# A fused attention, mixture-of-experts and MLP kernel: exponentials written in place, low parts on GpSimd with waits, joined flat copies, and the first entry's coarse values by four products each

## The chip, the cores and the metric

One NeuronCore of a Trainium2 chip runs the whole program in one launch. The metric is the device time of that launch in microseconds. Three runs of the kernel before gave 1092.92, 1094.10 and 1094.66 us; the median is 1094.1 us. The profile shown below is one further execution.

## The reference, cut to what matters

```python
def _attn_ref(q, k, v):                       # 2 x 8 x 576 x 64
    q_d, k_d, v_d = (x.reshape(B, H, S // 4, 4, D).mean(axis=3) for x in (q, k, v))
    out_up = np.repeat(sm_attn(q_d, k_d, v_d), 4, axis=2)      # coarse
    scores = np.where(abs(i - j) < 4, scale * q @ k.T, -1e9)   # local
    return out_up + softmax(scores) @ v

def _moe_ref(x, w_gate, w1, w2):              # 1152 x 512, 8 experts, 1024 wide
    P = exp(x @ w_gate - max); eight rounds of row and column normalisation
    return sum(P[:, e:e + 1] * (np.maximum(x @ w1[e], 0) @ w2[e]) for e in range(8))

def _moe2_ref(x, w_in, w_out):                # 512 -> 2048 -> 512
    h = x @ w_in
    return (maximum(h, 0) + log1p(exp(-abs(h)))) @ w_out
```

The three are chained: the attention's output, laid out as 1152 tokens of 512, goes through the experts and then through the MLP. The MLP's weights come as 64-bit floats and are taken apart by integer operations on the chip.

## The kernel before, in words

**Attention.** The 16 pairs of batch entry and head are worked in eight units of two heads (`units`, L452): four for the first entry (`self.b == 0`), then four for the second. A unit has four blocks: "c" (the coarse attention, all of it) and 0, 1, 2 (a third of the local attention each). The loop at L741 walks over the stream of 32 blocks: `scores` of block n, then `turn` (transposes of the exponentials) of block n-2, then `values` of block n-3. At the third and fourth block of a unit, `setup` (L313) of the next unit runs: nine TensorE transposes of q and k, sums of four neighbours for the coarse q and k (L327), the scaled coarse q (`flat`, L333, two pieces for each of three groups), and copies into `kT` and `fine`. After the last of them, `load` issues the q, k, v transfers of the unit after that, all on SyncE's one queue. The tile of q and k (`qk`) and that of v for the coarse part (`vd`) have one buffer each, so a load waits until the last reader of the unit before is done.

**Coarse values.** In `setup`, for every unit, GpSimd adds the four neighbours of v (L346, L347) into `vs`, and `values("c")` (L413) multiplies the turned exponentials with `vs`, in two halves of the 144 coarse keys and for two heads: four products. The two heads go to different halves of the output's partitions.

**Exponentials.** In `scores` ScalarE reads a block's scores from PSUM, writes the exponentials to a tile `ex` in SBUF and their sums to `rs` in SBUF (L379, three a block); VectorE adds a small constant to the sums (L380), inverts them (L381) and multiplies `ex` in place (L382).

**Expert weights.** Each float32 weight or activation is split into a high and a low part, and a product is made of three products of parts. The first layer goes by a scheme of seven products in place of eight, so that for each weight tile four sums of weights are needed (`weight_sums`, L105) as well as the plain pieces. `fetch_first` (L113) loads a tile into `raw` (two buffers for all weight loads), ScalarE writes the high parts, VectorE the low parts of the plain pieces (L133), GpSimd the four sums (L111) and their low parts (L139). `fetch_second` (L141) does the second layer's, with the low parts on GpSimd (L154). The first three pairs of fetches (f = 0, 1, 2) fall into the attention stage (L747), the rest are spread over the expert stage.

**Experts beside attention, and after it.** From the second entry's units on, the first four steps of the first expert (`beside`, L714) are woven in between the blocks. After the attention, TensorE's order is fixed by hand (L791); the other engines' order, and everything in the attention stage, is set by a scheduler from the dependencies. Later on `convert` (L161) makes the MLP's weights float32 and uses the same `weight_sums`.

## Time and profile before

| | |
|---|---|
| median of three runs | 1094.1 us |
| profiled execution, span from first to last instruction | 1094.7 us |
| TensorE busy | 1060.0 us (97%) |
| VectorE busy | 727.0 us (66%) |
| ScalarE busy | 555.2 us (51%) |
| GpSimd busy | 537.6 us (49%) |
| mean granted TensorE clock | 0.979 |

The profiled execution's only recorded time is its span, 1094.7 us; it is 0.6 us over the median of the runs and 0.04 us over the longest of them. All times below are microseconds from the span's start. [...] In the stretches from 160 us on TensorE is busy nearly all the time. It is not so before 90 us, which is the attention of the first batch entry.

### The profile page before, as it was taken

To read this page: it belongs to the slowest core of one execution; us is meant where nothing else is said; L and a number is where in the kernel's file an instruction comes from. 1 tells how busy PE (TensorE), PEld (TensorE's weight loads), DVE (VectorE), ACT (ScalarE), POOL (GpSimd) and SP (SyncE) were. 2 spreads that over 40 slices of the span, in tenths; PEclk is the share of its full clock that TensorE was granted. 3 is DMA by queue.
4 is the path that set the end of the run, shared out by engine and by line. 5 is a ranking of instruction groups with operands and counts; after the bars stand their busy time and mean duration, and the time that the engine had idled before them with its cause. 6 is when DMAs were issued, how large, how long until landed. Compare 5 with 4: busy or idle time off the path is not lost.

```text
span 1094.7 us, 17873 instructions
## 1 busy us (share of the span) xinstructions
PE 1060.0 (97%) x6385; PEld 938.0 (86%) x6385; DVE 727.0 (66%) x1532; ACT 555.2 (51%) x1443; POOL 537.6 (49%) x569
## 2 busy tenths in 40 slices
PE   6899999999999999999999999999999998999998
PEld 5678888998987889888888988898898897889987
DVE  6889665565666676667657665766663578766765
ACT  4667645343444444434444443444443567676763
POOL 6735235464467676756766455354664212222321
PEclk9579999999999999999999999999999999999999
DMA  8454101111235334434443332223333273244112
GB/s 175 118 115 109 49 27 55 62 58 40 84 100 145 115 110 143 132 105 127 122 134 102 117 112 93 100 93 110 102 116 116 106 278 139 113 175 182 68 39 87
DMA packets 133497, 119.70 MB, mean 109 GB/s; under 512 B 35744, under 2 KB 111776, under 8 KB 133408
## 3 DMA queue, kind: packets, MB, share of 16 engines
q1 hardware_dynamic: 133408, 118.56, 35.0%
q8 instruction: 50, 0.82, 0.3%
q14 instruction: 39, 0.32, 0.1%
HBM read 93.11 MB, written 25.43 MB: 108 GB/s over the span
## 4 chain that ended last, share of the span: by engine, by line
PE 40%; POOL 5%; DMA 5%; DVE 3%; issue 2%; ACT 2%; SPq 0%; POOLq 0%; ACTq 0%; DVEq 0%
PE yps L660 21%; PE m L601 19%; DMA raw<-in_moe_w_out 2%; POOL sums L111 2%; POOL w2l L154 1%; POOL cva L188 1%; POOL cva L197 1%; DMA raw<-in_moe_w 1%; DMA raw<-in_moe_w_in 1%; DVE cva L178 1%; POOL w1l L139 1%; DVE cva L189 0%; DVE cva L179 0%; DVE cva L182 0%; DMA s_out<-cva 0%
## 5 line engine op out<-in xcount | busy, mean ns | idle before, releaser
L601 PE MATMUL m<-xh,w1h 128*128 128x320 f32 (+1 forms) x1120 | 336.6, 301 | 13.1 <-ACT t L610 6.3
L601 PE MATMUL m<-xh,w1l 128*128 128x320 f32 (+1 forms) x1120 | 332.5, 297 | 0.0
L601 PE MATMUL m<-xl,w1h 128*128 128x320 f32 (+1 forms) x1120 | 332.4, 297 | 0.0
L601 PEld LDWEIGHTS m<-xh,w1h 128*128 128x128 f32 x1120 | 212.2, 189 | 38.7 <-ACT t L610 10.8
L601 PEld LDWEIGHTS m<-xl,w1h 128*128 128x128 f32 x1120 | 212.4, 190 | 11.8
L601 PEld LDWEIGHTS m<-xh,w1l 128*128 128x128 f32 x1120 | 212.2, 190 | 0.2 <-issue 0.2
L660 PE MATMUL yps<-w2h,hh 128*128 128x512 f32 x502 | 198.5, 395 | 0.0
L660 PE MATMUL yps<-w2l,hh 128*128 128x512 f32 x502 | 198.4, 395 | 0.0
L660 PE MATMUL yps<-w2h,hl 128*128 128x512 f32 x502 | 195.5, 389 | 0.0
L660 PE MATMUL yps<-w2h,h 128*128 128x512 f32 x436 | 153.3, 393 | 0.0
L615 DVE TENSOR_TENSOR c<-m,t 128x256 f32<-128x256 f32 (+1 forms) x160 | 72.3, 452 | 100.9 <-PE m L601 99.5
L139 POOL TENSOR_TENSOR w1l<-sums,w1h 128x512 fp32r<-128x512 f32 x72 | 95.8, 1345 | 78.2 <-ACT w1h L138 54.4
L571 POOL TENSOR_TENSOR ab<-ab,up 128x320 f32<-128x320 f32 (+1 forms) x64 | 53.9, 843 | 157.2 <-ACT ln L567 109.8
L154 POOL TENSOR_TENSOR w2l<-raw,w2h 128x512 fp32r<-128x512 f32 x72 | 94.9, 1339 | 71.4 <-ACT w2h L153 71.3
L558 ACT ACTIVATE hh<-c 128x256 fp32r<-128x256 f32 (+1 forms) x138 | 60.0, 443 | 125.0 <-DVE c L615 123.3
L559 DVE SCALAR_TENSOR_TENSOR hl<-c,hh 128x256 fp32r<-128x256 f32 (+1 forms) x138 | 91.4, 668 | 35.0 <-ACT hh L558 33.2
L660 PEld LDWEIGHTS yps<-w2h,hl 128*128 128x128 f32 x502 | 94.4, 188 | 21.3
L677 DVE SCALAR_TENSOR_TENSOR acc<-yps,pr,acc 128x512 f32<-128x512 f32 x117 | 86.9, 743 | 29.5 <-PE yps L660 29.4
L660 PEld LDWEIGHTS yps<-w2h,hh 128*128 128x128 f32 x502 | 94.7, 189 | 12.6 <-DVE acc L673 0.2
L660 PEld LDWEIGHTS yps<-w2l,hh 128*128 128x128 f32 x502 | 94.7, 189 | 11.1 <-issue 0.4
L660 PEld LDWEIGHTS yps<-w2h,h 128*128 128x128 f32 x436 | 82.6, 189 | 14.8
L188 POOL TENSOR_TENSOR cva<-cva,raw 128x512 uint32<-128x512 uint32 x32 | 42.7, 1336 | 95.2 <-DVE raw L185 76.6
(134 smaller groups left out, 1700.7 us busy)
## 6 DMA issues: line engine op xcount, KB each, us to landing
raw<-in_moe_w SPq DMA_DIRECT2D x72, 256.0 KB
raw<-in_moe_w SPq DMA_DIRECT2D x36, 512.0 KB
w1h<-s_in SPq DMA_DIRECT2D x10, 896.0 KB
w1l<-s_in SPq DMA_DIRECT2D x10, 896.0 KB
raw<-in_moe_w_in SPq DMA_DIRECT2D x32, 256.0 KB
raw<-in_moe_w_out SPq DMA_DIRECT2D x16, 512.0 KB
w2l<-s_out SPq DMA_DIRECT2D x10, 512.0 KB
w2h<-s_out SPq DMA_DIRECT2D x10, 512.0 KB
```

Of the source, the lines that this page charges most:

```text
L111: nc.gpsimd.tensor_tensor(sums[i], a, b, op=op)
L139: nc.gpsimd.tensor_tensor(lo[:, part], sums, hi[:, part].bitcast(F32), op=ALU.subtract)
L154: nc.gpsimd.tensor_tensor(lo[:, i], raw[:, i], hi[:, i].bitcast(F32), op=ALU.subtract)
L178: nc.vector.tensor_scalar(a, high, 0x07FFFFFF, 3, op0=ALU.bitwise_and, op1=ALU.logical_shift_left)
L188: nc.gpsimd.tensor_tensor(a, a, low, op=ALU.add)
L558: nc.scalar.activation(hh, c, AF.Relu)
L559: nc.vector.scalar_tensor_tensor(out=hl, in0=c, scalar=0.0, in1=hh.bitcast(F32), op0=ALU.max, op1=ALU.subtract)
L571: nc.gpsimd.tensor_tensor(ab, ab, up, op=ALU.subtract)
L601: nc.tensor.matmul(b[:, :h], x[:, i, kk, :], y[s][:, i, kk, :], start=(not more and n == 0), stop=(n == 5), skip_group_check=more,)
L615: nc.vector.tensor_tensor(c, b[:, :h], t, op=ALU.add)
L660: nc.tensor.matmul(y, a[:, f, tok], b[:, f, :], start=(start and m == 0), stop=(stop and m == 5))
L677: nc.vector.scalar_tensor_tensor(out=acc[t], in0=y, scalar=pr[:, t, e : e + 1], in1=acc[t], op0=ALU.mult, op1=ALU.add,)
```

## The change: what it does

- **Exponentials in place.** ScalarE writes the exponentials back to the PSUM bank of the scores, and their sums to three spare columns of the same bank. VectorE reads both from PSUM: the sum plus constant (L380) and the multiplication (L382), which now goes from PSUM to `ex` in SBUF.
- **Low parts on GpSimd.** For the first three fetches the low parts of the plain pieces (L133) go from VectorE to GpSimd.
- **Waits.** The helper `after` makes every GpSimd instruction of a fetch, or of a set of sums, depend on the one before it in a list, so that it waits for its completion.
- **Joined flat copies.** The six pieces of `flat` become two, made after the third group.
- **Coarse values.** For the first entry's four units the GpSimd sums are left out; `values("c")` takes the four neighbours of `vd` as they are, with sixteen products in place of four.

```diff
+    def after(chain, ins):
+
+        if chain:
+            tc.add_manual_dep(
+                ins.ins, chain[-1], mybir.DependencyInfo(mybir.DependencyClass.Sync, mybir.DependencyReason.DATA)
+            )
+        chain.append(ins.ins.name)
+
+    def weight_sums(sums, w, chain):
...
-            nc.gpsimd.tensor_tensor(sums[i], a, b, op=op)
+            after(chain, nc.gpsimd.tensor_tensor(sums[i], a, b, op=op))
...
+        chain = []
         for part, src in (
...
             nc.scalar.copy(hi[:, part], src)
-            nc.vector.tensor_tensor(lo[:, part], src, hi[:, part].bitcast(F32), op=ALU.subtract)
+            low = (nc.gpsimd if f < 3 else nc.vector).tensor_tensor(
+                lo[:, part], src, hi[:, part].bitcast(F32), op=ALU.subtract
+            )
+            if f < 3:
+                after(chain, low)
...
-            nc.gpsimd.tensor_tensor(lo[:, part], sums, hi[:, part].bitcast(F32), op=ALU.subtract)
+            after(chain, nc.gpsimd.tensor_tensor(lo[:, part], sums, hi[:, part].bitcast(F32), op=ALU.subtract))
...
-            nc.gpsimd.tensor_tensor(lo[:, i], raw[:, i], hi[:, i].bitcast(F32), op=ALU.subtract)
+            after(chain, nc.gpsimd.tensor_tensor(lo[:, i], raw[:, i], hi[:, i].bitcast(F32), op=ALU.subtract))
...
-            for hh in range(2):
+            for hh in range(2 if g == NB - 1 else 0):
                 half = slice(hh * D, (hh + 1) * D)
                 nc.vector.tensor_scalar(
-                    self.flat[half, g, hh].rearrange("x (j g) -> x j g", j=NB), qkd[half, tiles, 0],
+                    self.flat[half, :, hh].rearrange("x i (j g) -> x i j g", j=NB),
+                    qkd[half, :, 0].rearrange("x (i j) g -> x i j g", i=NB),
                     SCALE / (R * R), None, op0=ALU.mult,
                 )
...
-            if g:
+            if g or self.b == 0:
                 return
...
+            total = sc[:rows, NB * SD : NB * SD + NB].rearrange("p (i s) -> p i s", s=1)
             for i in range(NB):
-                nc.scalar.activation(ex[:, i], scv[:, i], AF.Exp, bias=off[:, i], accum_out=rs[:, i])
-            nc.vector.tensor_scalar(rs, rs, EPS, None, op0=ALU.add)
+                nc.scalar.activation(scv[:, i], scv[:, i], AF.Exp, bias=off[:, i], accum_out=total[:, i])
+            nc.vector.tensor_scalar(rs, total, EPS, None, op0=ALU.add)
             nc.vector.reciprocal(rs, rs)
-            nc.vector.tensor_tensor(ex, ex, rs.to_broadcast([rows, NB, w]), op=ALU.mult)
+            nc.vector.tensor_tensor(ex, scv, rs.to_broadcast([rows, NB, w]), op=ALU.mult)
...
-                    for c in range(2):
+                    terms = [
+                        (c, self.vd[:, c, hh, r] if self.b == 0 else self.vs[:, c, hh])
+                        for c in range(2) for r in range(R if self.b == 0 else 1)
+                    ]
+                    for n, (c, vals) in enumerate(terms):
                         nc.tensor.matmul(
-                            pv[hh * D : (hh + 1) * D, :SD], self.vs[:, c, hh],
+                            pv[hh * D : (hh + 1) * D, :SD], vals,
```

The scheduler orders the attention stage anew. On SyncE's queue (`qk`, `vw`, `vd` are a unit's q and k, its windows of v and its v for the coarse part; `raw` is expert weights) the kernel before has, from the load for the third unit's coarse v to that of the fifth unit's q:

```order
L311 DMA vd<-in_v 72x2x256
L298 DMA qk<-in_q 64x9x64 x2
L298 DMA qk<-in_k 64x9x64 x2
L311 DMA vd<-in_v 72x2x256
L124 DMA raw_1207<-in_moe_w 128x4x128 x2
L124 DMA raw_1258<-in_moe_w 128x4x128 x2
L304 DMA vw<-in_v 72x2x64 x2
L308 DMA vw<-in_v 72x7x64 x2
L311 DMA vd<-in_v 72x2x256 x2
```

and the changed kernel, for the same stretch, where L132, L312, L318, L322 and L325 are the lines that were L124, L298, L304, L308 and L311:

```order
L132 DMA raw_1262<-in_moe_w 128x4x128 x2
L312 DMA qk<-in_q 64x9x64 x2
L312 DMA qk<-in_k 64x9x64 x2
L318 DMA vw<-in_v 72x2x64 x2
L322 DMA vw<-in_v 72x7x64 x2
L132 DMA raw_1482<-in_moe_w 128x4x128 x2
L325 DMA vd<-in_v 72x2x256 x2
```

The fourth unit's q and k, which stood ahead of the third and fourth weight loads (raw_1207, raw_1258), now stand behind both (raw_1262 is the second of them), and the third unit's coarse v behind a fifth.

On TensorE the kernel before has, around the second unit's products (L413; L322 are the transposes of `setup`, L355 the coarse scores, L402 the turning of the local exponentials):

```order
L322 MATMUL tb<-ident,qk 128x128 x3
L413 MATMUL pv<-etc,vs 64x144
L402 MATMUL tp<-ident,ex 72x128 x3
L413 MATMUL pv<-etc,vs 64x144 x3
L362 LDWEIGHTS identb
L362 MATMUL sc<-mask,identb 128x216
L355 MATMUL sc<-qkd,flat_149 96x144 x2
```

and the changed kernel, around the second unit's sixteen products (L433, before L413; L336 are the transposes of `setup`, before L322; L370 the coarse scores; L444 the local values):

```order
L370 MATMUL sc<-qkd,flat_149 96x144 x3
L418 MATMUL tp<-ident,ex 72x128 x3
L377 LDWEIGHTS identb
L377 MATMUL sc<-mask,identb 128x216
L383 MATMUL sc<-kT,fine_147 128x72 x3
L433 MATMUL pv<-etc,vd 64x144 x16
L336 MATMUL tb<-ident,qk 128x128 x6
L444 MATMUL pv<-et,vw 64x64 x6
```

The products of the second unit now stand behind the third unit's coarse scores (L370), and directly ahead of the fourth unit's transposes; before they stood ahead of those scores.

On GpSimd the kernel before works the second fetch (raw_778 the first layer's tile, w2l<-raw_969 the second layer's) so:

```order
L111 TENSOR_TENSOR sums<-raw_778 128x256 x2
L347 TENSOR_TENSOR vs<-vd 72x128 x2
L111 TENSOR_TENSOR sums<-raw_778,sums 128x256
L154 TENSOR_TENSOR w2l<-raw_969,w2h 128x512 x2
L111 TENSOR_TENSOR sums<-raw_778,sums 128x256
```

and the changed kernel (raw_977 is now the second layer's) so:

```order
L142 TENSOR_TENSOR w1l<-raw_778,w1h 128x256
L152 TENSOR_TENSOR w1l<-sums,w1h 128x512
L142 TENSOR_TENSOR w1l<-raw_778,w1h 128x512
L168 TENSOR_TENSOR w2l<-raw_977,w2h 128x512
L119 TENSOR_TENSOR sums<-raw_778 128x256
L168 TENSOR_TENSOR w2l<-raw_977,w2h 128x512
L119 TENSOR_TENSOR sums<-raw_778 128x256
L119 TENSOR_TENSOR sums<-raw_778,sums 128x256 x2
```

The two low parts that were VectorE's (L142) now stand ahead of the sums of the tile (L119), which are its last readers; the sums of v (L347) are gone.

## Rows read from the trace of the kernel before

**Rows 1.** Page, costliest groups: form and count, then busy us, mean ns, idle before.

```profile
L139 POOL TENSOR_TENSOR w1l<-sums,w1h 128x512 fp32r<-128x512 f32 x72 | 95.8, 1345 | 78.2 <-ACT w1h L138 54.4
```

**Rows 2.** Windows: stretch, length, busy (instructions) of PE, PEld, DVE, ACT, POOL, clock, DMA.

```profile
25.20:32.00 6.80, 5.52 (x67) 4.54 (x66) 6.56 (x20) 5.53 (x26) 6.80 (x9) 1.00 0.66 179
32.00:66.20 34.20, 29.91 (x175) 23.82 (x175) 29.99 (x78) 21.46 (x84) 22.33 (x28) 0.50 0.61 127
66.20:79.80 13.60, 11.54 (x124) 10.03 (x123) 9.16 (x35) 9.99 (x46) 1.88 (x4) 0.99 0.48 92
79.80:86.60 6.80, 6.55 (x35) 5.86 (x36) 6.71 (x24) 3.51 (x14) 1.40 (x2) 0.52 0.34 77
86.60:160.00 73.40, 72.46 (x608) 61.71 (x606) 56.01 (x148) 48.30 (x175) 31.82 (x32) 1.00 0.26 64
160.00:900.00 740.00, 730.07 (x4235) 651.05 (x4234) 467.30 (x864) 324.71 (x731) 406.50 (x400) 1.00 0.34 109
```

**Rows 3.** Waits from 0 to 110 us: who waited for whom, us, times, longest.

```profile
PE tp L393 <- DVE ex L382: 3.3, 3, 2.2
PE tp L402 <- DVE ex L382: 1.3, 2, 1.1
PE tp L402 <- DVE small L380: 1.3, 1, 1.3
```

**Rows 4.** Timeline of PE: start, us, engine, line, operation, idle before.

```profile
19.82 1.24 PE L413 MATMUL pv<-etc,vs 72*64 72x144 f32 x8
...
46.62 1.49 PE L322 MATMUL tb<-ident,qk 128*128 128x128 f32 x6
...
63.40 1.49 PE L322 MATMUL tb<-ident,qk 128*128 128x128 f32 x6
...
70.19 0.72 PE L413 MATMUL pv<-etc,vs 72*64 72x144 f32 x8
...
78.43 0.85 PE L322 MATMUL tb<-ident,qk 128*128 128x128 f32 x6 [2.06 <-DMA qk<-in_k]
```

**Rows 5.** Lines by form, DVE, 19 to 66 us: busy us, mean ns.

```profile
L382 DVE TENSOR_TENSOR ex<-ex,small 128x216 f32<-128x216 f32 x9 | 8.0, 901 | 0.1
...
L133 DVE TENSOR_TENSOR w1l<-raw,w1h 128x256 fp32r<-128x256 f32 x3 | 3.8, 1252 | 0.0
L380 DVE TENSOR_SCALAR small<-small 128x3 f32<-128x3 f32 x8 | 3.4, 424 | 0.0
L382 DVE TENSOR_TENSOR ex<-ex,small 96x432 f32<-96x432 f32 x3 | 3.1, 1022 | 0.1
...
L133 DVE TENSOR_TENSOR w1l<-raw,w1h 128x512 fp32r<-128x512 f32 x3 | 2.4, 798 | 0.0
L439 DVE TENSOR_TENSOR xf<-pv,xc 128x192 f32<-128x192 f32 x7 | 2.4, 339 | 1.4 <-PE pv L424 1.3
```

**Rows 6.** Timeline of DVE: the same multiplication twice.

```profile
33.54 3.70 DVE L382 TENSOR_TENSOR ex<-ex,small 128x216 f32<-128x216 f32 x1
...
39.53 0.37 DVE L382 TENSOR_TENSOR ex<-ex,small 128x216 f32<-128x216 f32 x1
```

**Rows 7.** Timeline of POOL: a run at 34 us, and sums without and with waits.

```profile
33.83 2.48 POOL L154 TENSOR_TENSOR w2l<-raw,w2h 128x512 fp32r<-128x512 f32 x2
...
388.08 1.44 POOL L111 TENSOR_TENSOR sums<-raw 128x256 f32<-128x256 f32 x2 [2.12 <-DMA s_in<-cva]
389.48 1.56 POOL L111 TENSOR_TENSOR sums<-raw,sums 128x256 f32<-128x256 f32 x2
```

**Rows 8.** Timeline of SP: issues of transfers.

```profile
35.45 1.28 SPq L298 DMA_DIRECT2D qk<-in_q  x2
...
38.83 2.04 SPq L124 DMA_DIRECT2D raw<-in_moe_w  x4
...
71.57 1.29 SPq L298 DMA_DIRECT2D qk<-in_q  x2
```

**Rows 9.** Timeline of ACT: an instruction and one that waits for it.

```profile
891.18 0.47 ACT L564 ACTIVATE ab<-c 128x320 f32<-128x320 f32 x1 [0.99 <-DVE c L615]
891.69 0.47 ACT L565 ACTIVATE ab<-ab 128x320 f32<-128x320 f32 x1
```

More of the change, by code (lines that the diff above doesn't have):

```diff
@@ L103, in attention_moe_mlp @@
     weights = {}
-    def weight_sums(sums, w):
+    def after(chain, ins):
[5 more added lines that the diff above has]
+    def weight_sums(sums, w, chain):
         for i, a, b, op in (
@@ L132, in fetch_first @@
             nc.scalar.copy(hi[:, part], src)
-            nc.vector.tensor_tensor(lo[:, part], src, hi[:, part].bitcast(F32), op=ALU.subtract)
+            low = (nc.gpsimd if f < 3 else nc.vector).tensor_tensor(
[3 more added lines that the diff above has]
+                after(chain, low)
         two = [smp.tile([P, 2, 2, P], F32, tag="sums", name="sums") for _ in range(2)]
-        weight_sums([two[i // 2][:, i % 2] for i in range(SUMS)], lambda fh, d: raw[:, d, :, fh, :])
+        weight_sums([two[i // 2][:, i % 2] for i in range(SUMS)], lambda fh, d: raw[:, d, :, fh, :], chain)
         for i, sums in enumerate(two):
@@ L151, in fetch_second @@
         nc.sync.dma_start(raw, w2[e].rearrange("(h a p) d -> p h a d", h=2, p=P)[:, :, p, :])
+        chain = []
         for i in range(2):
             nc.scalar.copy(hi[:, i], raw[:, i])
-            nc.gpsimd.tensor_tensor(lo[:, i], raw[:, i], hi[:, i].bitcast(F32), op=ALU.subtract)
+            after(chain, nc.gpsimd.tensor_tensor(lo[:, i], raw[:, i], hi[:, i].bitcast(F32), op=ALU.subtract))
     TINY = 2.0 ** -15 * 1.125
@@ L210, in convert @@
         sums = smp.tile([P, SUMS, P], F32, tag="sums", name="sums")
-        weight_sums([sums[:, i] for i in range(SUMS)], lambda fh, d: a[:, 2 * d + fh])
+        weight_sums([sums[:, i] for i in range(SUMS)], lambda fh, d: a[:, 2 * d + fh], [])
         parts(sums, first[:, :SUMS], nc.gpsimd)
@@ L411, in values @@
                 for hh in range(2):
-                    for c in range(2):
+                    terms = [
[3 more added lines that the diff above has]
+                    for n, (c, vals) in enumerate(terms):
                         nc.tensor.matmul(
-                            pv[hh * D : (hh + 1) * D, :SD], self.vs[:, c, hh],
+                            pv[hh * D : (hh + 1) * D, :SD], vals,
                             et[:, c].rearrange("s (i h q) -> s i h q", i=NB, h=2)[:, :, hh],
-                            start=(c == 0), stop=(c == 1),
+                            start=(n == 0), stop=(n == len(terms) - 1),
                         )
```

## The prediction

> **What bounds the kernel now.** I read the stretches first, because the shares of the whole span hide where TensorE has room. From 160 to 900 us it is busy for 730.1 of 740.0 us, and from 86.6 to 160 for 72.5 of 73.4, at the full clock [rows 2]: there nothing that other engines do can give back more than a few microseconds. Room is before 86.6 us, in the first entry's four units. There the clock matters as much as the gaps. From 25.2 to 32.0 it was granted in full; then, after TensorE had waited 2.2 us in one piece for VectorE's multiplication of the exponentials [rows 3], it stood at half from 32.0 to 66.2, though TensorE was busy for 29.9 of those 34.2 us; and it fell again at 79.8, after a wait of 2.06 us for q and k [rows 2, 4]. The waits say what was late: TensorE's transposes waited for L382 and L380 on VectorE, 3.3 + 1.3 + 1.3 = 5.9 us in all [rows 3].
>
> Why is VectorE late? The same multiplication took 3.70 us at 33.54 and 0.37 us at 39.53 [rows 6]. During the first, GpSimd ran without a break, two low parts of 2.48 us among them [rows 7]. Nine of these took a mean of 901 ns, three coarse ones 1022, and eight additions to three numbers 424 ns each, while a VectorE operation that reads its tensor from PSUM beside one in SBUF (L439) kept to 339 ns in the same stretch [rows 5]. So VectorE loses time where it works on SBUF alone while GpSimd does.
>
> **In-place exponentials.** Twelve multiplications took 8.0 + 3.1 = 11.1 us between 19 and 66 us. Undisturbed they would take 9 x 0.37 + 3 x 0.74 (the coarse ones have twice the columns) = 5.6. Reading PSUM they should not be disturbed, as L439 is not, so 5.5 us go. Eight additions of 3.4 us drop at least to 8 x 0.34 = 2.7, another 0.7 [rows 5]. The cost is on ScalarE: three exponentials of a block share one bank now, and two of the three wait for the one before. A waiting instruction starts 0.51 us after the start of one that takes 0.47 [rows 9], so a wait costs 0.04 us and the overlap of neighbours; I bound it by 0.04 and 0.3 (most of a short instruction), 8 a unit, 0.3 to 2.4 us, and take 1. The bank of scores is also held until VectorE has multiplied; with three banks in turn I cost that at nothing, and its cover is that a bank comes round again only three blocks later.
>
> **Low parts on GpSimd.** VectorE loses 3.8 + 2.4 = 6.2 us over three fetches [rows 5]. GpSimd gains 0.72 us for the narrow one (half of 1.44 [rows 7]) and 1.35 for the wide one [rows 1], 2.07 a fetch. Together with the last part, VectorE is rid of 5.5 + 0.7 + 6.2 = 12.4 us in 47, which is 2.8 units of 16.8 us (63.40 less 46.62 [rows 4]), so 4.4 us a unit. It had 29.99 of 34.2, or 14.7 a unit [rows 2], and comes to 10.3. The joined flat copies take a little more off; I put them at nothing, since VectorE is then not the last.
>
> As disturbed as it is here, VectorE needed 1.25 + 0.80 = 2.05 us for the two [rows 5], just what GpSimd needs. [...]
>
> **The waits on GpSimd.** Two sums without a wait between took 1.44 us, two with one 1.56 [rows 7], so a wait costs 0.12 us. Some 120 are new over the whole program, about 15 us of an engine that is half idle. Behind it TensorE is full [rows 2]; I take 0, with ends of -1 (breaks that VectorE can use) and +2.
>
> **Sixteen products.** Eight passes (four products) took 1.24 us at the lower clock and 0.72 at the higher [rows 4]. The difference, 0.52, is their streaming at the full clock, and 0.2 is latency. Sixteen take 4.2 us at half and 2.1 at full, so a unit gains 3.1 or 1.6 us of TensorE, if the two heads still run side by side as in that row, where they write different halves of the partitions; if not, 7.3 or 3.6. I take side by side. What goes in return, the sums of v on GpSimd, nobody on TensorE waited for long.
>
> **The pace of a unit.** ScalarE needs 21.46 / 34.2 x 16.8 = 10.5 us plus 1. TensorE needs 29.91 / 34.2 x 16.8 = 14.7 at half, 17.8 with the products; at full half of 14.7 plus 1.6, 8.9 [rows 2]. So at the higher clock a unit could take 11.5 (ScalarE), at the lower 17.8 (TensorE). The long waits for VectorE ahead of the fall of the clock go, and a block of 4 us without gaps comes in, so I expect the higher clock most of the time: with a third of the units' time at half, 17.8 / 3 + 11.5 x 2 / 3 = 13.6 in place of 16.8.
>
> **The queue it is moved past.** The fourth unit's q and k, issued at 35.45 ahead of the weights at 38.83 [rows 8], now stand behind those weights, whose buffer is free only when GpSimd has read the second weight tile. If GpSimd is no later than before they issue at 38.83 + 2.04 = 40.9; with two fetches' low parts (4.1) and eight waits (1.0) more, at 46.0; the dropped sums of v give some back, so I take 42.5. From issue to use such a load took 78.43 - 71.57 = 6.9 us when TensorE waited for it [rows 4, 8]. So these transposes come at 49.4 (bounds 47.8 and 52.9) where they stood at 46.62, 2.8 us later. From there the pace of 13.6 gives the fifth unit's at 63.0 (before 63.40) and the sixth's at 76.6 (before 78.43), 1.8 us ahead. From then on TensorE has the experts' products beside and is the bound; so what is gained there stays.
>
> **Sum.** Sixth unit -1.8; the second fall of the clock at 79.8, which cost half of 6.55 us busy [rows 2], 3.3, goes if the wait for q and k ahead of it does, and I take -3; waits 0. That is -4.8 on the span of 1094.7, 1089.9; the median of the runs lies 0.6 lower, so **1089 us**, with 1085 to 1092 as this case's own range.
>
> **Rivals.**
> 1. *Slower: the clock stays at half and the added products are the path.* Eight tenths of the stretch from 32.0 to 66.2 was busy TensorE at half [rows 2], and the clock did not rise for being busy. Then a unit takes 17.8: the sixth unit's transposes come at 49.4 + 35.6 = 85.0, 6.6 us late, giving 1100; if the two heads run one after the other, 22 a unit, 1109. It decides if the clock is at half for more than about two thirds of the time from 32 to 66 us. Against it: the longest waits go.
> 2. *No change: the load queue takes the place of VectorE.* With GpSimd slower at its new work, weight buffers come free late, and q, k and v stand behind them on the one queue: TensorE waits for transfers where it waited for VectorE. At the late bound, 52.9, and 13.6 a unit, the sixth unit's come at 80.1, 1.7 late, against a smaller loss of clock: 1094. For it: 2.06 us were waited for a q and k load already [rows 4]. [...]
> 3. *A larger gain.* The clock stays up from 25 us on and the queue is not late: 46.6 + 2 x 11.5 = 69.6, 8.8 us early, and 3.3 for the later fall: 1082.
> 4. *It does not do what it says:* the exponentials' waits on each other and the banks held longer take from ScalarE and TensorE what VectorE gains; about 1095.
>
> **Chances.** A measurement of this kernel tells about 0.2%, 2.2 us, from no change. Forecast 0.42, larger gain 0.14, the queue 0.20, the clock at half 0.20, not as it says 0.04. Faster: 0.42 + 0.14 + 0.03 (the better edge of the queue's case) = 0.59; the same: most of the queue's and the last case, 0.19; slower: 0.22. The range goes from the larger gain, 1082, to the clock's case, 1100; outside are some of both ends, under 0.2 in all.
>
> **What would show it.** Right: L382 near 0.4 us throughout the attention stage and no wait of TensorE for it over 1 us; more than half of 32 to 66 us at the higher clock; the sixteen products in some 2 us at the higher clock; the sixth unit's transposes near 77 us. Wrong: TensorE waiting for q, k or `vd` transfers for several us before 60 (second rival), or busy at half to 66 us and beyond (first rival), or a stretch after 160 us that differs by over 2 us, which I have at nothing.

## The result, and the profile after

The changed kernel is slower: 1106.4 us (median of four runs, 1099.81 to 1114.35) beside 1094.4 for the kernel before, a ratio of 1.0109 (95%: 1.0083 to 1.0136). Six later runs gave 1.0082 (1.0050 to 1.0115). Ratios rest on fast runs alone and are not quotients of the medians beside them, which take in every run. I had 1089, with 1100 as the upper end. Not only the middle moved: the runs spread over 14.5 us where those of the kernel before spread over 4.4.

The profiled run happens to be the fastest of the four (1099.81, span 1098.0), so it shows what the change does at its best. Measured times stand 1.8 us above the span in every run; the profiled execution of before was therefore one of 1096.5, 2.4 above the median shown, not 0.6 as I had put it.

Totals on the page of the changed kernel:

```profile
PE 1062.6 (97%) x6481; PEld 942.4 (86%) x6481; DVE 706.5 (64%) x1494; ACT 557.8 (51%) x1443; POOL 540.6 (49%) x559
```

VectorE is rid of 20.5 us (727.0 before), TensorE has 96 instructions more (6385 before). The same stretches as in [rows 2], columns as there:

```profile
25.20:32.00 6.80, 6.80 (x31) 5.46 (x31) 0.00 (x0) 2.37 (x6) 4.69 (x5) 1.00 0.67 169
32.00:66.20 34.20, 30.04 (x289) 26.78 (x290) 23.66 (x83) 26.49 (x111) 18.80 (x20) 0.95 0.57 127
...
79.80:86.60 6.80, 6.60 (x69) 5.42 (x67) 6.12 (x18) 5.25 (x20) 3.20 (x5) 1.00 0.71 156
...
160.00:900.00 740.00, 727.07 (x4208) 647.32 (x4207) 468.49 (x858) 323.20 (x724) 415.37 (x400) 1.00 0.34 107
```

VectorE fell from 29.99 to 23.66 us between 32 and 66 us, as intended. But TensorE was busy for 6.80 of 6.80 us from 25.2 on, and VectorE did nothing there at all: TensorE's own work holds up the rest. The fall of the clock at 80 us is gone (1.00 where [rows 2] have 0.52). Between 160 and 900 us it has 3.0 us less work done than before.

TensorE's timeline of the changed kernel (start, us, line, operation; in brackets the idle time ahead) shows what that work is:

```profile
23.49 2.18 PE L433 MATMUL pv<-etc,vd 72*64 72x144 f32 x8
...
26.39 5.12 PE L433 MATMUL pv<-etc,vd 72*64 72x144 f32 x24
...
44.00 1.48 PE L370 MATMUL sc<-qkd,flat 128*96 128x144 f32 x6 [2.25 <-DVE flat L347]
...
46.09 1.43 PE L383 MATMUL sc<-kT,fine 128*128 128x72 f32 x6
47.45 3.83 PE L433 MATMUL pv<-etc,vd 72*64 72x144 f32 x32
51.20 0.87 PE L336 MATMUL tb<-ident,qk 128*128 128x128 f32 x6
...
53.29 0.80 PE L383 MATMUL sc<-kT,fine 128*128 128x72 f32 x6
...
59.07 3.70 PE L433 MATMUL pv<-etc,vd 72*64 72x144 f32 x32
62.70 0.87 PE L336 MATMUL tb<-ident,qk 128*128 128x128 f32 x6
...
70.78 3.70 PE L433 MATMUL pv<-etc,vd 72*64 72x144 f32 x32
77.09 0.87 PE L336 MATMUL tb<-ident,qk 128*128 128x128 f32 x6
```

The sixteen products (32 passes, L433) took 2.18 + 5.12 = 7.3 us in the first unit and 3.70 in the third and fourth. I had 4.2 and 2.1. The longest wait between 20 and 110 us is a new one, 2.25 us for the joined flat copy (L347). The six products of `kT` (L383) are a clock to read by: 1.43 us at the lower level, 0.80 at the higher. That is needed, since the first record of the clock in this trace stands at 34.1 us and is one of the higher level; ahead of it the clock column says 1.00, as it does for 25.2 to 32.0, though the products of `kT` took 1.43 us just ahead of that stretch, at 21.49, and the coarse scores (L370) at its end, at 31.44, took 1.76, beside 0.98 at 57.10.

Two numbers per trace carry the rest: **H**, how long the clock stood at its lower level up to 168 us (all of the time ahead of the first record, checked by those products, and the records after it), and **E**, the start of the 223rd product of the experts' first line (L601 before, L621 after), behind which every kernel has the same TensorE work in the same order. Span less E is what a profile took for that work. For the kernel before H is 66 us and E 168.7; for this profile of the change 37 and 166.0.

### The profile page after: what moved, and what is told of

Its sections match the earlier page's. It is cut to its first block, busy times and chain, and to the rows that moved or that the text cites. A ratio compares the mean times of both kernels' runs of the same rounds, so it can differ in the third digit from the quotient of the medians.

```text
span 1098.0 us, 18045 instructions
## 1 busy us (share of the span) xinstructions
PE 1062.6 (97%) x6481; PEld 942.4 (86%) x6481; DVE 706.5 (64%) x1494; ACT 557.8 (51%) x1443; POOL 540.6 (49%) x559
## 4 chain that ended last, share of the span: by engine, by line
PE 55%; POOL 12%; DVE 8%; DMA 6%; issue 5%; ACT 3%; SPq 1%; POOLq 0%; DVEq 0%; ACTq 0%
PE yps L680 27%; PE m L621 25%; POOL sums L119 5%; DMA raw<-in_moe_w_in 2%; POOL w2l L168 2%; POOL cva L211 2%; DMA raw<-in_moe_w_out 2%; DVE cva L193 2%; POOL w1l L152 1%; POOL cva L202 1%; DVE cva L203 1%; DMA raw<-in_moe_w 1%; DVE cva L196 1%; DVE hl L579 1%; DMA s_in<-cva 1%
## 5 line engine op out<-in xcount | busy, mean ns | idle before, releaser
L621 PE MATMUL m<-xh,w1h 128*128 128x320 f32 (+1 forms) x1120 | 337.0, 301 | 16.6 <-ACT t L630 8.9
L621 PE MATMUL m<-xl,w1h 128*128 128x320 f32 (+1 forms) x1120 | 332.7, 297 | 0.0
L621 PE MATMUL m<-xh,w1l 128*128 128x320 f32 (+1 forms) x1120 | 332.0, 297 | 0.0
L621 PEld LDWEIGHTS m<-xh,w1h 128*128 128x128 f32 x1120 | 212.3, 190 | 43.5 <-ACT t L630 12.9
L621 PEld LDWEIGHTS m<-xl,w1h 128*128 128x128 f32 x1120 | 212.5, 190 | 11.8
L621 PEld LDWEIGHTS m<-xh,w1l 128*128 128x128 f32 x1120 | 212.3, 190 | 0.3 <-issue 0.2
L152 POOL TENSOR_TENSOR w1l<-sums,w1h 128x512 fp32r<-128x512 f32 x72 | 101.2, 1406 | 60.8 <-ACT w1h L151 32.5
L579 DVE SCALAR_TENSOR_TENSOR hl<-c,hh 128x256 fp32r<-128x256 f32 (+1 forms) x138 | 86.7, 632 | 40.6 <-ACT hh L578 38.5
L680 PE MATMUL yps<-w2l,h 128*128 128x512 f32 x218 | 86.1, 395 | 0.0
```

The lines of the kernel that those rows point to most:

```text
L152: after(chain, nc.gpsimd.tensor_tensor(lo[:, part], sums, hi[:, part].bitcast(F32), op=ALU.subtract))
L579: nc.vector.scalar_tensor_tensor(out=hl, in0=c, scalar=0.0, in1=hh.bitcast(F32), op0=ALU.max, op1=ALU.subtract)
L621: nc.tensor.matmul(b[:, :h], x[:, i, kk, :], y[s][:, i, kk, :], start=(not more and n == 0), stop=(n == 5), skip_group_check=more,)
L680: nc.tensor.matmul(y, a[:, f, tok], b[:, f, :], start=(start and m == 0), stop=(stop and m == 5))
```

## Experiments

Each ratio is to runs of the kernel before on the same chip. Their median was 1096.9 us for no_waits, sums_back, heads_in_turn and sums_back_no_waits; 1096.2 for products_alone, exps_flat, waits_alone and change_again; 1097.0 for waits_early, waits_late, change_early_waits and before_again; 1097.2 for half_products, products_alone_turn, low_alone and no_products_early; 1096.9 for fewer_buffers and v_twice. H and E, in us, are of one profiled execution each.

| kernel | median us | ratio (95%) | H | E |
|---|---|---|---|---|
| before_again | 1096.4 | 0.9995 (0.9974 to 1.0016) | 65 | 167.5 |
| change_again | 1106.1 | 1.0082 (1.0050 to 1.0115) | 52 | 174.8 |
| no_waits | 1118.6 | 1.0218 (1.0179 to 1.0258) | 79 | 190.1 |
| sums_back | 1099.8 | 1.0031 (1.0012 to 1.0050) | 77 | 168.2 |
| sums_back_no_waits | 1099.7 | 1.0025 (1.0001 to 1.0049) | 55 | 166.7 |
| heads_in_turn | 1107.1 | 1.0105 (1.0070 to 1.0140) | 51 | 170.6 |
| products_alone | 1119.7 | 1.0204 (1.0154 to 1.0255) | 68 | 180.6 |
| products_alone_turn | 1109.3 | 1.0101 (1.0043 to 1.0158) | 75 | 179.7 |
| exps_flat | 1097.9 | 1.0005 (0.9987 to 1.0023) | 63 | 167.7 |
| low_alone | 1104.7 | 1.0066 (1.0043 to 1.0090) | 71 | 174.3 |
| waits_alone | 1106.2 | 1.0083 (1.0056 to 1.0110) | 76 | 171.9 |
| waits_early | 1102.6 | 1.0070 (1.0043 to 1.0098) | 71 | 170.4 |
| waits_late | 1099.0 | 1.0017 (1.0005 to 1.0030) | 69 | 167.5 |
| change_early_waits | 1107.1 | 1.0067 (1.0024 to 1.0110) | 56 | 175.8 |
| no_products_early | 1098.4 | 1.0016 (0.9993 to 1.0038) | 54 | 166.0 |
| half_products | 1107.5 | 1.0093 (1.0062 to 1.0124) | 48 | 170.7 |
| fewer_buffers | 1104.7 | 1.0081 (1.0052 to 1.0110) | 43 | 168.1 |
| v_twice | 1107.7 | 1.0107 (1.0074 to 1.0139) | 45 | 169.4 |

**Undoing one part: no_waits, sums_back, sums_back_no_waits.** The waits off, the products off, both off:

```diff
-        if chain:
+        if False:
```
```diff
-            if g or self.b == 0:
+            if g:
...
-                        (c, self.vd[:, c, hh, r] if self.b == 0 else self.vs[:, c, hh])
-                        for c in range(2) for r in range(R if self.b == 0 else 1)
+                        (c, self.vs[:, c, hh])
+                        for c in range(2) for r in range(1)
```

> The changed kernel without the added waits on GpSimd; all else as changed. Theory of the waits: the 6 us that TensorE loses against the kernel before between 316 and 660 us (from 2.7 us ahead to 3.3 us behind, at the same products) come from sums and low parts on GpSimd that arrive 0.1 us later each, so they go: span 6 us under the changed kernel's at the same clock, about 1100 us median. Rival, the order: the scheduler's new order of ScalarE, VectorE and GpSimd costs it, waits or not: TensorE still falls back by 4 us or more in that stretch, and the median stays near 1106.

> The changed kernel with the coarse values of the first entry from GpSimd sums and four products again; in-place exponentials, low parts, waits and joined copies stay. Theory of the products: the sixteen products run one after the other (3.70 us of TensorE a unit at the higher clock, 7.3 at the lower, against 0.72 and 1.24 for four), and where the clock is late this multiplies; so the spread of the runs (1100 to 1114) goes and the median falls by 8 to 12 us to 1094 to 1098. Rival, the sums: GpSimd with sums and low parts both is the later one, the weights come late and the median stays within 4 us of 1106.

> Neither sixteen products nor added waits: in-place exponentials, low parts on GpSimd and joined flat copies alone. If both theories hold, the two losses add up: about 6 us under the run with the sums back, 1088 to 1092, faster than the kernel before. If the waits are what keeps VectorE from GpSimd's long runs, it is no better than with them.

Without the waits the kernel is slower still, which neither of my theories had: so the waits are not what the change pays for as a whole. With the sums back it comes within 0.3% of the kernel before, with the waits or without, and not under it, as I had expected without them (1088 to 1092). The products carry most of the loss.

**The two heads in turn: heads_in_turn.** The same sixteen products, with the head as the inner loop:

```diff
-                for hh in range(2):
-                    terms = [
...
-                    for n, (c, vals) in enumerate(terms):
+                terms = [(c, r) for c in range(2) for r in range(R if self.b == 0 else 1)]
+                for n, (c, r) in enumerate(terms):
+                    for hh in range(2):
...
```

> The changed kernel with the sixteen products written in turn for the two heads, one of each, in place of eight and eight. If the two halves of the output run side by side when they stand next to each other: 1.9 to 2.2 us of TensorE a unit at the higher clock in place of 3.70, the median 5 to 8 us lower, about 1100. Rival, it is the count of passes that matters and not their order: 3.7 us again and 1106.

The products became shorter, as expected; the kernel did not become measurably faster, where I had expected 1100. How short, at the higher clock (heads_in_turn, TensorE's timeline):

```profile
71.20 2.18 PE L431 MATMUL pv<-etc,vd 72*64 72x144 f32 x32
```

**One part alone: products_alone, products_alone_turn, exps_flat, low_alone, waits_alone.** Each is the kernel before with one part of the change (exps_flat with two, the in-place exponentials and the joined flat copies); products_alone_turn has the loop order above. The diff for low_alone, the others being pieces of the change's own:

```diff
-            nc.vector.tensor_tensor(lo[:, part], src, hi[:, part].bitcast(F32), op=ALU.subtract)
+            (nc.gpsimd if f < 3 else nc.vector).tensor_tensor(lo[:, part], src, hi[:, part].bitcast(F32), op=ALU.subtract)
```

> Edit: the kernel before with one part of the change, the sixteen products a unit in place of the sums of v for the first entry; no waits, no moved low parts, exponentials and flat copies as before. Theory 'the products are serial': the two heads' products run one after the other, 3.7 us a unit at the higher clock and 7.3 at the lower, against 0.72 and 1.24 for four products before. Before, the stretch from 32 to 66 us stood at half, so with the products as the only edit most units meet the lower clock: about 6 us a unit of TensorE over two to three units, of which part hides in the waits for VectorE; 1103 to 1112 for a kernel before at 1096 to 1097. Rival 'the products cost only in the package' (they hurt because the other parts let TensorE run ahead): within 0.2% of the kernel before.

> Edit: the kernel before with the sixteen products alone, the two heads in turn product by product, so that the two write different halves of the partitions side by side (4.8 us a unit at the lower clock in the changed kernel with the same edit, against 7.3). Theory 'serial products are the loss': against 1119.7 with the heads one after the other, four units with 2.5 us less at the lower clock, 1.2 at the higher, 5 to 10 us less: 1110 to 1115. Rival 'the order is the loss, not the products' time': 1117 to 1122.

> Edit: the kernel before with the in-place exponentials and the joined flat copies alone; low parts stay on VectorE, no waits on GpSimd, sums of v as before. Theory 'VectorE was worth what I said, the products ate it': the exponentials' multiplications at 0.37 us and the units' pace under 16 us, sixth unit's transposes 1 to 3 us earlier, 1092 to 1095 for a kernel before at 1096 to 1097. Rival 'what is gained before 160 us is waited away behind it': the products of the experts at 168 us 1 to 3 us earlier, at the end within 1 us, ratio within 0.998 to 1.002.

> Edit: the kernel before with the low parts of the first three weight tiles on GpSimd, without waits, alone. Theory 'VectorE's time in the attention stage is not what sets the end' (as the in-place exponentials alone showed): ratio 0.997 to 1.003. Rival 'GpSimd is the dearer engine for them': weight buffers come free late and the load queue waits, 1.003 to 1.010.

> Edit: the kernel before with the waits between GpSimd's instructions alone. Theory 'the waits set another order in the expert stage': nothing changes before 150 us beyond 1 us, and TensorE's gaps between 316 and 425 us grow from 2.7 us to 4 to 5.5 as in the three kernels that have the waits; ratio 1.001 to 1.003. Rival 'the waits cost nothing by themselves': gaps there under 3.5 us, ratio 0.998 to 1.001. A second rival, that breaks on GpSimd free VectorE: multiplications of L382 shorter than 3 us and the end 1 to 3 us earlier.

The products alone cost 2.0%, more than the whole change and than I had expected; in turn, half of that, though the two intervals, of four runs each, just touch. Products of one unit at the lower clock, of products_alone and then of products_alone_turn (TensorE's timelines):

```profile
39.95 7.04 PE L417 MATMUL pv<-etc,vd 72*64 72x144 f32 x32
```
```profile
62.15 4.11 PE L415 MATMUL pv<-etc,vd 72*64 72x144 f32 x32
```

So 4.2 and 2.1 were right for products whose heads take turns (4.11 and 2.18); the change issues one head's eight and then the other's, 7.04 and 3.70. In these runs, then, the neighbour in program order decided the time; by what means no run takes apart.

The in-place exponentials and joined copies alone give nothing (1.0005), and the low parts alone cost 0.66%, where I had expected 0.3 at most. VectorE's groups between 19 and 66 us (busy us, mean ns), of exps_flat, low_alone and the changed kernel:

```profile
L142 DVE TENSOR_TENSOR w1l<-raw,w1h 128x256 fp32r<-128x256 f32 (+1 forms) x6 | 9.3, 1565 | 2.1 <-ACT w1h L141 2.0
L396 DVE TENSOR_TENSOR ex<-sc,small 128x216 f32<-128x216 f32 (+1 forms) x12 | 5.1, 427 | 0.1
```
```profile
L380 DVE TENSOR_SCALAR small<-small 128x3 f32<-128x3 f32 (+1 forms) x10 | 12.0, 1200 | 0.0
L382 DVE TENSOR_TENSOR ex<-ex,small 128x216 f32<-128x216 f32 (+1 forms) x11 | 6.7, 614 | 0.1
```
```profile
L398 DVE TENSOR_TENSOR ex<-sc,small 128x216 f32<-128x216 f32 (+1 forms) x11 | 4.7, 429 | 0.0
...
L396 DVE TENSOR_SCALAR small<-sc 128x3 f32<-128x3 f32 (+1 forms) x13 | 1.9, 149 | 1.8 <-ACT sc L395 1.8
```

The time that VectorE lost beside GpSimd went, in these profiles, to instructions that still read SBUF alone, though not to all of them: the reciprocals, which do too, kept to a mean of 168 ns in exps_flat and in the changed kernel. With the exponentials in PSUM the six low parts took 9.3 us where they had taken 6.2 [rows 5]; with the low parts away a three-column addition took a mean of 1200 ns, both forms together, in place of 424 for the wider one. In the changed kernel, which has both, neither is disturbed (429 and 149 ns).

**Waits by stage: waits_early, waits_late, change_early_waits, and before_again.** The waits only in the first three fetches, or only from the fourth on and in the conversions; the changed kernel with the early ones only; the kernel before once more. The edit for the early ones (the conversions have none then either):

```diff
-        chain = []
+        chain = [] if f < 3 else None
```

> Edit: the kernel before, with waits between GpSimd's instructions only where they belong to the expert stage (fetches from the fourth weight tile on, and the conversions); the instruction order of every engine before 150 us is that of the kernel before, and from 300 to 700 us ScalarE, VectorE and GpSimd get the order that the changed kernel has there. Theory 'the waits' order costs in the expert stage': TensorE's gaps between 316 and 425 us grow from 2.7 to 4 to 5.5 us, one gap near 485 us of about 2 us, ratio 1.002 to 1.005. Rival 'the 10 us of the waits alone are all of the attention stage': ratio 0.998 to 1.002 and gaps as in the kernel before.

> Edit: the kernel before, with the waits only in the fetches of the first three weight tiles; behind 160 us the orders are those of the kernel before but for some 30 rows near 900 us. Theory 'in the attention stage the waits set another order, under which TensorE stands at the lower clock for longer': half clock for more than 66 us in all before 100 us (products of q and kT 0.21 us apart in place of 0.11), ratio 1.003 to 1.008. Rival 'the waits cost in the expert stage only': ratio 0.998 to 1.002. A third possibility, that breaks on GpSimd let VectorE through: faster, 0.995 to 0.998, with the multiplications of L382 under 3 us.

> Edit: the changed kernel without the waits of the expert stage; the order of every engine there is that of the kernel before. Theory 'the waits' order costs in the expert stage': 2 to 5 us less than the changed kernel (1106), so 1101 to 1104, and TensorE's gaps between 316 and 425 us near 3 us in place of 5.5. Rival 'the expert stage takes back whatever was gained ahead of it': 1105 to 1108, gaps there as in the changed kernel.

> The kernel before once more, unaltered, for a second profile: how far its own progress and clock vary. Theory 'without the sixteen products the clock of the first 90 us hardly matters': whatever its half-clock time before 90 us, the experts' products stand at 168 us within 2 us of the first profile. Rival 'the first profile was a lucky one': progress at 168 us, or the loss behind it, like that of the changed kernel (over 3 us later at the end).

The waits alone came at 1.0083, where I had expected 1.003 at most. The early waits alone cost 0.70%, at E (+1.7 in the profile, H 71) and again near 940 us (+2); the late ones 0.17%, none of it ahead of 300 us. Within the change, taking the late ones away moved nothing that can be told (1107.1 beside 1106.1), where I had expected 2 to 5 us, so there their size stays open; what they do can be seen. With the sixteen products the waits as a whole do not cost but save: 1118.6 us without them, 1106.1 with all, 1107.1 with the early ones only. Of nine profiled executions with the late waits, eight have a fall of the clock for 3.4 us between 316 and 520 us; of eleven without them, none. In the changed kernel it stands at 488 us, behind the longest gap of the stage, 2.13 us at 484.8. ScalarE there (timeline):

```profile
482.19 0.43 ACT L578 ACTIVATE h<-m 128x320 fp32r<-128x320 f32 x1
485.93 0.62 ACT L151 CAST w1h<-sums 128x512 fp32r<-128x512 f32 x1 [3.31 <-POOL sums L119]
486.45 0.75 ACT L630 COPY t<-m 128x320 f32<-128x320 f32 x2
```

and GpSimd:

```profile
480.86 1.55 POOL L211 TENSOR_TENSOR sums<-sums,raw 128x512 fp32r<-128x512 f32 x1
484.37 1.53 POOL L119 TENSOR_TENSOR sums<-raw 128x256 f32<-128x256 f32 x2 [1.96 <-DMA s_in<-cva]
485.98 1.53 POOL L119 TENSOR_TENSOR sums<-raw,sums 128x256 f32<-128x256 f32 x2
```

The order that the scheduler made with the waits puts a conversion right ahead of the fetch, so GpSimd's sums wait 1.96 us for the conversion's buffer to be written out. ScalarE's cast waits 3.31 us for the sums, and behind the cast stands the copy `t` that TensorE needs. TensorE's waits between 316 and 430 us, most of them for `t`, `u` and the sums `c` made with them, of the changed kernel:

```profile
PE m L621 <- ACT t L630: 2.7, 2, 1.5
PE m L621 <- DVE c L635: 2.1, 3, 1.1
PE m L621 <- ACT u L630: 0.6, 2, 0.3
```

and of the kernel before:

```profile
PE m L601 <- DVE c L615: 1.0, 1, 1.0
PE m L601 <- ACT t L610: 0.9, 1, 0.9
PE m L601 <- DVE hl L559: 0.4, 1, 0.4
```

before_again is the measure for all such differences: it stood 1.2 us ahead of its own first profile at E and 1.3 behind at the end, so two profiles of one program differ by 2.5 us behind 168 us.

**What remains without the products: no_products_early.** The changed kernel with the sums back and the early waits only (both diffs above).

> Edit: the changed kernel with the sums of v put back and without the waits of the expert stage, so in-place exponentials, joined flat copies, low parts on GpSimd and the waits of the first three fetches. Theory 'serial products and late waits are the loss': the fall of the clock near 490 to 515 us goes, progress at 168 us as in the kernel before or 1 to 2 us ahead, 1094 to 1098 beside 1096 to 1097, ratio 0.998 to 1.002. Rival 'the early waits cost here as they do alone': 1.004 to 1.008.

E is 166.0, 1.5 us ahead of before_again, and 1.0016 at the end: nothing gained, and the early waits' 0.7% is not paid beside the other two parts.

**Fewer products, and more room for v: half_products, fewer_buffers, v_twice.** Eight products a unit in place of sixteen (GpSimd keeps the first of its two sums, an edit not shown); then, with two other buffers cut to make room, v in one buffer or two:

```diff
-            if g or self.b == 0:
+            if g:
...
-                        for c in range(2) for r in range(R if self.b == 0 else 1)
+                        for c in range(2) for r in range(2 if self.b == 0 else 1)
```
```diff
-            self.vd = vd = ap.tile([HC, 2, 2, R, D], F32, tag="vd", bufs=1, name="vd")
+            self.vd = vd = ap.tile([HC, 2, 2, R, D], F32, tag="vd", bufs=2, name="vd")
```

> Edit: the changed kernel with eight products a unit in place of sixteen: GpSimd makes the first of the two sums of v, and the two halves are added up on TensorE. Theory 'the serial products at a clock that varies are the loss': 8 products take about 1.9 us a unit at the higher clock and 3.7 at the lower, half of what is added, so half of the difference between the changed kernel (1106) and the one with the sums put back (1100): 1101 to 1105. Rival 'what counts is the order that the scheduler sets when v waits for TensorE' (one buffer of v, held until the products are done): as the changed kernel, 1105 to 1109.

> Edit: the changed kernel with two buffers in place of three for the multiplied exponentials and one in place of two for the sums of v, which makes room for the next kernel; a control. Expected of both theories: within 4 us of the changed kernel, 1103 to 1111 beside a kernel before at 1097.

> Edit: fewer_buffers with two buffers in place of one for v of a unit, which the products read and so hold until TensorE has done them; the load queue waited for that for 16.6 us in the changed kernel between 10 and 90 us. Theory 'the held buffer of v stops the load queue, and that is why eight products cost as much as sixteen': the queue's waits on the products go, and the kernel is 3 to 7 us below fewer_buffers. Rival 'TensorE at the lower clock is the bound, the loads are in time anyway': within 2.5 us of fewer_buffers.

Eight products took 1.71 and 1.91 us in the two units at the higher clock and cost as much as sixteen, so my theory in its simple form, time on TensorE alone, fell here. But TensorE then waited longer for other things than in the change, whose longest wait there was 2.25 us (waits of half_products between 20 and 110 us):

```profile
PE tp L419 <- DVE ex L399: 4.1, 1, 4.1
PE tb L336 <- DMA qk<-in_k: 3.0, 1, 3.0
PE tp L410 <- DVE ex L399: 2.4, 2, 1.7
```

The load queue did wait for the products (waits of the queue between 10 and 90 us, of fewer_buffers and of v_twice):

```profile
SPq L325 <- PE pv L433: 12.8, 4, 5.7
```
```profile
SPq L325 <- PE pv L433: 6.8, 4, 5.0
```

but with half of that gone the kernel was no faster; the other half was not tried. In the profiles of the change and of v_twice TensorE waited for no transfer between 20 and 110 us, so there the queue does not hold it.

## Why the prediction was wrong

**The step that failed: "if the two heads still run side by side ... I take side by side".** They don't in the order in which the loop issues them: 3.70 and 7.04 us, so a unit gains 3.0 and 5.8 us of TensorE (over 0.72 and 1.24 [rows 4]), where I took 1.6 and 3.1 and had 3.6 and 7.3 written down for the other case. I chose by the four products of before, where the second head follows after only two of the first. That row was too short to decide. The dearer products show from the first unit on: the third unit's transposes came at 34.59 and 35.35 us in the two profiles of the change, at 28.19 and 29.45 in those of the kernel before. But this term does not carry the whole miss: with the heads in turn, at the lengths I had put down, the change still stood at 1.0105. (Those lengths, 4.2 and 2.1, leave out the 0.2 us of latency that I had just estimated from [rows 4]; that changes nothing.)

**The second: the clock, which goes with the size.** Among the kernels with sixteen products head by head, E rises with H almost on a line: 37 us at the lower clock and 166.0, 43 and 168.1, 45 and 169.4, 52 and 174.8, 56 and 175.8, 68 and 180.6, 79 and 190.1, that is (190.1 - 166.0) / (79.4 - 37.5) = 0.57 us for each at the lower level, with points up to 2.8 off the line; an engine without a gap would pay 0.5, an estimate from the granted 0.50 [rows 2]. Work drawn out at the lower level lengthens H too, so the line shows that the two go together and not which comes first. Among those without products the low end is flat: H of 54, 55, 63, 65, 66, 69 and 77 gave 166.0, 166.7, 167.7, 167.5, 168.7, 167.5 and 168.2. (Three one-part kernels lie above: 170.4 to 174.3 at 71 to 76.) At nearly the same H, sums_back had 168.2 and no_waits 190.1. So in the kernel before the lower clock cost next to nothing; with the products TensorE is the bound by these numbers, as I feared in the first rival, and a run pays by the clock it was granted. The runs say the same without a trace: the ten of the change lie at 1097.4 us plus 0.86 for each 0.001 that the mean clock is below 1 (correlation -0.96), the 82 of the kernel before beside the experiments at 1096.2 plus 0.05 (correlation -0.17). (A mean clock leaves out what was granted ahead of the first record.) change_early_waits had two runs with a mean clock of 1.000, 1096.3 and 1099.1 us, beside 1107.1 to 1108.6 for the other three.

Where the clock fell is visible in three profiles of the change (two of it, one of change_early_waits): at 44.3, 45.7 and 46.0 us, up to 1.6 us behind the end of the wait for the joined flat copy, which took 2.25, 2.22 and 2.25 us. In fewer_buffers that wait was 2.03 us, and no fall followed. Falls also stand beside such waits in two kernels without the products: at 55.9 us behind one of 1.96 (exps_flat), and at 40.6 within one of 3.06 (no_products_early). In the kernel before TensorE waited for no flat copy there. I had put the joined copies at nothing; I did not undo them alone, so that they bring the fall is argued, not shown.

Shorter products fit that picture only when compared at equal H: heads_in_turn and products_alone_turn lie about 3 and 8 us under the line, half_products about 1, and only the 8 is more than the line's own scatter. Why the clock did not rise sooner or stay up with them is open; their gain in the median was nothing, except without the other parts (1119.7 to 1109.3). Nor does E hold all of their loss: span less E was 937.2 us in heads_in_turn and 934.3 in half_products, beside 926.0 and 928.5 in the two profiles of the kernel before.

**Waits at nothing.** Wrong in kind. What one wait takes was not the cost: a wait changes the order that the scheduler makes on all engines. Alone the waits cost 10 us, beside the products they save 12; and the late ones bring a gap and a fall of the clock, at half for 3.4 us. How much of the loss behind 168 us is theirs is open. Span less E was 932.0 and 933.5 us in the profiles of the change, so 3.5 to 7.5 more than in those of the kernel before; but it was nearly as much, or more, without the late waits (931.0 in change_early_waits, 931.8 in no_products_early, 932.7 in no_waits, 933.1 in products_alone, 934.1 in sums_back_no_waits), and only 929.3 with them alone (waits_late). No run isolates that part. A stretch behind 160 us that differs by over 2 us was on my list of what would prove me wrong.

**The gains, -1.8 and -3, did not come either.** Without the products, no_products_early stood at 1.0016 and sums_back_no_waits at 1.0025. The second fall of the clock, which I priced at 3 us, is not the kernel's but the execution's: before_again, the same program as before, has none there,

```profile
79.80:86.60 6.80, 5.87 (x45) 4.34 (x47) 6.67 (x26) 5.58 (x25) 1.17 (x3) 1.00 0.53 119
```

and it was 1.2 us earlier at E and 1.3 later at the end. So "what is gained there stays" failed as well.

**What was right.** The multiplications and additions went to the lengths I gave (429 ns as a mean of both forms, 149 ns), for the reason given, though the parts could not be priced one by one. The fourth unit's transposes came at 51.20 (49.4, bounds 47.8 and 52.9), the fifth's at 62.70 (63.0), the sixth's at 77.09 (76.6), and the fall of the clock at 80 us went. That holds for a run in which the clock was at half for 5.5 us from 32 to 66 us; I had a third of the time. In change_again it was 20.5 us (up to the first record at 35.4, and 17.1 from 45.7 on), and the fourth unit came at 55.33, the sixth at 84.15. So even the right milestones were one draw. Nor did they buy what I said: 2.7 us at E in the best profile, where no_products_early, without any products, had the same 166.0. That a block of TensorE work without gaps brings the higher clock, on which I rested the third of the time, no run shows: in products_alone the clock was 0.50 from 66.2 to 79.8 us with TensorE busy for 13.60 of 13.60.

**The rivals.** The first came nearest: TensorE and the products are the path, 22 us a unit with one head after the other at half, 1109. It has the runs between 1104 and 1114. Its condition, that the clock stand at half for two thirds of the stage, was a little too strict: 20.5 of the 34.2 us were enough in change_again. The second did not happen: TensorE waited for no transfer between 20 and 110 us in either profile of the change. But moving the low parts alone did cost something (low_alone, 1.0066), though GpSimd was hardly slower at them: four took it a mean of 1037 ns there, where VectorE's six, disturbed as they were, had taken 6.2 us [rows 5], 1033 each. With the exponentials in PSUM beside it, less is lost (sums_back_no_waits, 1.0025, 1.0001 to 1.0049). The third did not happen. The fourth's time, about 1095, is near that of the kernels without the products, but its reason, exponentials that wait for each other and banks held longer, no run isolates.

No version here beats the kernel before; the nearest is exps_flat, at 1.0005.

## What to carry to other kernels

Side by side on TensorE went, in these runs, by neighbouring instructions (3.70 us for eight products of each head in a row, 2.18 with the heads in turn): write the loop so that the halves take turns, and read the proof from a row with as many products as you mean to issue, and then time it, for here the shorter products gave nothing back in the median beside the other parts. Ask of an engine near its limit what it costs at its lower clock (7.04 us here where it was 3.70), not at the one of the profile. The stage with slack hid the clock in the seven kernels without the products named above, with E of 166.0 to 168.7 at H of 54 to 77 us, and a few microseconds of added work a unit turned run-to-run clock into run-to-run time, with E of 166.0 and 174.8 in two executions of the changed kernel. And under this scheduler a dependency added for one engine is a new program for all: compare the orders in every stage, also where nothing was meant to change.

## What I had not expected of the hardware

Time lost beside GpSimd was passed on here, not removed: a three-column addition on VectorE took a mean of 1200 ns in low_alone, against 149 in the changed kernel, where its input lies in PSUM. GpSimd's own low parts took a mean of 1037 ns in low_alone; whether the one length comes from the other no run shows.

The clock stayed at its lower level through long busy stretches: in products_alone it was 0.50 from 66.2 to 79.8 us, with TensorE busy for all 13.60, and in sums_back the products of `kT` still took 1.43 us at 62.82, with TensorE busy for 30.86 of the 34.20 us from 32.0 to 66.2. It differs between executions of one program: 37 and 52 us of H in the change's two profiles.
